# A fused attention and feed-forward block on one core: its calls written out as one list for all engines

## The chip, the cores and the metric

The kernel runs on one core of one Trainium2 chip. The metric is device microseconds of one execution, the median of the runs. A core has TensorE (matmuls; "PE", its weight loads "PEld"), VectorE ("DVE"), ScalarE ("ACT"), GpSimd ("POOL") and SyncE ("SP", which here only issues DMAs). Each engine runs its instructions in the order in which they were written and waits on semaphores for the others. Matmul results land in PSUM, from which VectorE or ScalarE copies them out.

## What is computed

One layer over S = 2048 rows of D = 640, 32 heads of 20 columns, FF = 1536, all in bf16. The inputs, cut to what matters:

```python
h  = x + attention(layernorm(x))
h2 = h + (gelu(n @ w_gate) * (n @ w_up)) @ w_down      # n = layernorm(h)

# attention of x (normalised):
q, k, v = split(x @ wqkv)                               # 32 heads of 20
pq, pk  = q @ w_phi, k @ w_phi                          # per head, 20 x 20
phi_q   = concat(softmax(pq), softmax(-pq))             # 40 features
phi_k   = concat(softmax(pk), softmax(-pk))
kv, z   = sum_s(phi_k^T v), sum_s(phi_k)
o       = (phi_q @ kv) / (phi_q @ z + 1e-6)
return o @ wo
```

## The kernel before

Rows are cut into 16 tiles of 128 (`t`), four tiles make a block (`b`), the 640 columns are five chunks of 128 (`c`).

**Start (lines 169 to 435).** x tiles 0 and 1 are loaded first, then W_v in three parts between the later x tiles. Nine matmuls on zeros warm TensorE up (`warm`, line 212), two more stand in between (`WA`). Each x tile has its mean and variance taken by `ln_stats` (two halves with bn_stats, then bn_aggr). Tiles 0 and 1 are only centred (`ln_0`, line 246): the factor 1/std goes into the later copies of v and into the exponential of k. Tile 3's sums come from ScalarE (`st3_act`). The first six tiles are transposed by TensorE (`transpose_to`, line 142), the others by a DMA transpose on SP's queue. `v_part` and `v_mm` make v; `fold` (line 214) multiplies W_k, and later W_q, with the 20 x 20 matrices of the heads, using the transposed weights that `load_T` fetches by DMA transpose.

**The k stage (lines 440 to 488).** For each tile: `k_tile` makes pk on TensorE and two exponentials (plus and minus) on ScalarE; `v_mm` makes v of tile t+4; `ln_ap` normalises tile t+6 and issues its DMA transpose; `k_norm` (line 310) sums the exponentials on VectorE, takes the reciprocal and multiplies v by it, once per sign, on GpSimd or VectorE (`VP` says which). `kv_tile` (line 334) adds k^T v of a tile into the PSUM tile `kvp`; `KVG` gathers the tiles 0-1, 2-5, 6-9, 10-11, and 12 to 15 follow behind the loop. Four q products stand at t = 15 (`QT`). `kv_mask` brings the sums, masked, into `KV`. PSUM is a pool of four slots at first, then of three and `kvp`.

**After it (lines 493 to 737).** `attn_a` makes numerators and denominators from the exponentials of q, `attn_b` to `attn_b3` divide them, `attn_t` transposes, `attn_c` multiplies with W_o, `attn_d` adds x and takes the sums for the second normalisation, `attn_e` normalises and transposes. `gate_up` makes one of twelve strips of the hidden layer, `down` the output. `weave` mixes the attention steps of later tiles into the list of strips by position.

The order on all engines is thus that of these loops and of `weave`. The first k product (line 274) and the first strip (line 618) are the marks used below.

Of the kernel before, what the change touches and what calls it, by code (L numbers as in the profile page):

```python
# [17 lines left out]
def kernel(  # L18
# [25 lines left out]

    H0 = [(P * c) // Dh for c in range(NC)]
    NH = [(P * c + P - 1) // Dh - H0[c] + 1 for c in range(NC)]
    NWARM = 9
    VP = (0, 2, 4, 6, 9, 11)
    KA, QA = (0, 2, 4), (0, 1, 2, 3, 4)
    FQ = (4, 6, 8, 10, 12)  # L50

    QG = ((0, 1), (2, 3), (4, 5), (6,), (7, 8), (9, 10), (11, 12), (13, 14), (15,), (16,), (17,), (18,), (19,))
    QT = (15, 15, 15, 15)
    WA = 2
    T3 = 4

    KVG = {5: (0, 1), 9: (2, 3, 4, 5), 13: (6, 7, 8, 9), 15: (10, 11)}
    VC = Dh + 1
    KC = Dh + 2


    UH = H // 2
    HALF = (slice(0, 64), slice(64, P))

# [4 lines left out]

    const = ctx.enter_context(tc.tile_pool(name="const", bufs=1))  # L70
    ps_cm = ExitStack()
    psG = ps_cm.enter_context(tc.tile_pool(name="psG0", bufs=4, space=PSUM, reuse_waits="tile"))
    ctx.enter_context(tc.manual_schedule(engines={nc.tensor.engine, nc.sync.engine}))
    man_cm = tc.manual_schedule()
    man_cm.__enter__()
# [6 lines left out]
    KV = const.tile([P, NC, 2, 4, KC], BF16, name="KV")  # L82

    Eq = [const.tile([P, len(g), 2, 512], BF16, name=f"Eq{j}") for j, g in enumerate(QG)]
# [6 lines left out]

    def eq(t, c, s):
        for E, g in zip(Eq, QG):
            if t // 4 * NC + c in g:
                return E[:, g.index(t // 4 * NC + c), s, t % 4 * P:(t % 4 + 1) * P]

    def small(pool, shape, name, bufs=3):
        return pool.tile(shape, F32, name=name, bufs=bufs)

    def gtile(name):  # L100
        return psG.tile([P, 2, 512], F32, name=name, tag="G")

    def ln_stats(pool, tiles, tag, act=True, between=None, log=False):

        n = len(tiles)
        mv = small(pool, [P, n, nc.vector.BN_AGGR_DIM], "mv" + tag)
        stats = small(pool, [P, n, 2, nc.vector.BN_STATS_DIM], "stats" + tag)
        for j, xt in enumerate(tiles):
            for i in range(2):
                nc.vector.bn_stats(stats[:, j, i, :], xt[:, i * HD:(i + 1) * HD])  # L110
                if between and i == j == 0:
                    between()
        for j in range(n):
            nc.vector.bn_aggr(mv[:, j, :], stats[:, j])
        ve = small(pool, [P, n], "ve" + tag)
        rstd = small(pool, [P, n], "rstd" + tag)
        if log:

            nc.scalar.activation(ve, mv[:, :, 1], ACTF.Ln, bias=eps)
            nc.scalar.activation(rstd, ve, ACTF.Exp, scale=-0.5)  # L120
        else:
            nc.gpsimd.tensor_scalar_add(ve, mv[:, :, 1], EPS)
            nc.gpsimd.tensor_tensor(rstd, ve, nhalf[:, 0:n], op=ALU.pow)

        mr = small(pool, [P, n], "mr" + tag)
        if act:
            for j in range(n):
                nc.gpsimd.tensor_scalar(mr[:, j:j + 1], mv[:, j, 0:1], rstd[:, j:j + 1], -1.0,
                                        op0=ALU.mult, op1=ALU.mult)
        return [(xt, mv[:, j, 0:1], rstd[:, j:j + 1], mr[:, j:j + 1]) for j, xt in enumerate(tiles)]  # L130

    def ln_act(pool, tag, xt, mean, rstd, mr):
        ln = pool.tile([P, D], BF16, name="ln" + tag, bufs=3)
        nc.scalar.activation(ln, xt, ACTF.Identity, bias=mr, scale=rstd)  # L134
        return ln

    def ln_dve(pool, tag, xt, mean, rstd, mr):
        ln = pool.tile([P, D], BF16, name="ln" + tag, bufs=3)
        nc.vector.tensor_scalar(ln, xt, mean, rstd, op0=ALU.subtract, op1=ALU.mult)  # L139
        return ln  # L140

    def transpose_to(dst, src, on_pe, on_dve=False):

        if on_pe:
            tp = psG.tile([P, 16, P], BF16, name="tp", tag="G")
            for c in range(NC):
                nc.tensor.transpose(tp[:, c, :], src[:, c * P:(c + 1) * P], ident)  # L147
            (nc.vector.tensor_copy if on_dve else nc.scalar.copy)(dst, tp[:, 0:NC, :])  # L148
        else:
            nc.sync.dma_start_transpose(dst, src)  # L150

# [9 lines left out]

    vS = [p1.tile([P, H, VC], BF16, name=f"vS{i}") for i in range(8)]
    fp_cm = tc.tile_pool(name="fp", bufs=1, side="right", reuse_waits="tile")
    fp = fp_cm.__enter__()
    WkT = fp.tile([P, NC, D], BF16, name="WkT")
    WqT = p1.tile([P, NC, D], BF16, name="WqT")


    nc.gpsimd.memset(nhalf, -0.5)
    nc.gpsimd.memset(eps, EPS)  # L170
    nc.sync.dma_start(x_sb[0][:, 0:1, :], x_v[:, 0:1, :])
    nc.sync.dma_start(x_sb[0][:, 1:2, :], x_v[:, 1:2, :])

    nc.scalar.add_instruction(mybir.InstLoadActFuncSet(name=nc.get_next_instruction_name(), act_func_set_id=6))
    nc.sync.dma_start(Wv[:, 0:2, :], w_v[:, 0:2, 2 * D:3 * D])
    nc.sync.dma_start(x_sb[0][:, 2:3, :], x_v[:, 2:3, :])
    nc.sync.dma_start(Wv[:, 2:4, :], w_v[:, 2:4, 2 * D:3 * D])
    nc.sync.dma_start(x_sb[0][:, 3:4, :], x_v[:, 3:4, :])
    nc.sync.dma_start(wphi, phi_v.rearrange("(c p) f -> p c f", p=P))
    nc.sync.dma_start(Wv[:, 4:5, :], w_v[:, 4:5, 2 * D:3 * D])  # L180
    nc.sync.dma_start(x_sb[1][:, 0:2, :], x_v[:, 4:6, :])

    def load_T(WT, i, *ds):

        for d in ds:
            nc.sync.dma_start_transpose(WT[:, :, d * P:(d + 1) * P], A_wqkv[d * P:(d + 1) * P, i * D:(i + 1) * D])

    load_T(WkT, 1, *range(NC))
    wo_v = A_wo.rearrange("(c p) n -> p c n", p=P)
    wg_v = B_w_gate.rearrange("(c p) n -> p c n", p=P)  # L190
    wu_v = B_w_up.rearrange("(c p) n -> p c n", p=P)


    zero = fp.tile([P, 512], BF16, name="zero")
    nc.vector.memset(zero, 0.0)
    for i in range(8):
        nc.vector.memset(vS[i][:, :, Dh], 1.0)
    make_identity(nc, ident)
    nc.gpsimd.memset(hmask, 1.0)
    for c in range(NC):  # L200
# [3 lines left out]
        nc.gpsimd.affine_select(out=hmask[:, c, :], in_=hmask[:, c, :], pattern=[[Dh, 8]],  # L204
                                compare_op=ALU.is_ge, fill=0.0, base=Dh - 1 - off, channel_multiplier=-1)

    wu = gtile("wu")
    def warm(n):
        for _ in range(n):
            nc.tensor.matmul(wu[:, 0, :], lhsT=zero[:, 0:P], rhs=zero, start=True, stop=True)  # L210

    warm(NWARM)

    def fold(WT, W2, halves, ds=range(NC)):


        runs = []
# [7 lines left out]
        for d in ds:  # L225
            wa = gtile("wa")
            for i, (u, c, a, b) in enumerate(runs):
                nc.tensor.matmul(wa[:, u, a - u * HD:b - u * HD], lhsT=WT[:, c, d * P:(d + 1) * P],  # L228
                                 rhs=BD[:, c].rearrange("p a b -> p (a b)")[:, a - H0[c] * Dh:b - H0[c] * Dh],
                                 start=(i == 0 or runs[i - 1][0] != u),  # L230
                                 stop=(i + 1 == len(runs) or runs[i + 1][0] != u), skip_group_check=True)
            dst, src = W2[:, d, :].rearrange("p (u f) -> p u f", u=2), wa[:, :, 0:HD]
            if halves:
                dst = W2[:, d, :].rearrange("p (c u f) -> p u c f", c=NC, u=2)
                src = src.rearrange("p u (c f) -> p u c f", c=NC)
            if d in (QA if halves else KA):
                nc.scalar.copy(dst, src)
            else:
                nc.vector.tensor_copy(dst, src)

    lnp, Ek, Vt = {}, {}, {}

    CT = (0, 1)
    nrstd = [p1.tile([P, 1], F32, name=f"nrstd{t}") for t in CT]

    def ln_0(t):
        xt, mean, rstd, _ = lnp[t] = ln_stats(p1, [x_sb[0][:, t, :]], f"c{t}", False, None, True)[0]
        nc.gpsimd.tensor_scalar(nrstd[t], rstd, -1.0, None, op0=ALU.mult)
        xc = fp.tile([P, D], BF16, name="xc", bufs=2)
        nc.vector.tensor_scalar(xc, xt, mean, None, op0=ALU.subtract)  # L250
        return xc

    def ln_st(*tiles, act=True, between=None, log=False):
        for t, v in zip(tiles, ln_stats(p1, [x_sb[t // 4][:, t % 4, :] for t in tiles], "1", act, between, log)):
            lnp[t] = v
# [512 lines left out]
```

## Time and profile before

| | |
|---|---|
| median of 3 runs (lowest to highest) | 278.62 us (278.49 to 278.63) |
| span of the profiled execution | 276.6 us |
| first TensorE matmul (warm-up) starts | 1.24 us |
| first transpose of an x tile starts | 5.05 us |
| first v matmul starts | 6.58 us |
| first k matmul starts | 16.99 us |
| last group of k^T v starts | 67.83 us |
| first strip of the hidden layer starts | 90.28 us |
| last store is issued by | 274.39 us |

The span runs from the first to the last instruction of the profiled execution; the time of a run holds what lies around it too, 2.0 us here. The page counts a matmul as busy from its start to its modelled end, so neighbours overlap: in a run of equal matmuls the step from start to start is the figure that adds up. The granted clock is 1.000 in every stretch asked for. An engine that is idle costs nothing unless TensorE, or the end, waits for it.

The large groups of the page, for later comparison: gate and up products 61.9 and 61.7 us busy (line 618), down products 53.8 (line 639), W_o, W_k and W_v products 24.3, 24.0 and 19.8, q products 22.9.

### The profile page before, as it was taken

What the parts mean: (1) busy time and instruction counts of PE and PEld (TensorE: products, weight loads), DVE (VectorE), ACT (ScalarE), POOL (GpSimd) and SP (SyncE); (2) the same over time, 40 slices, a digit from 0 to 9 for tenths busy, and PEclk for the clock granted to TensorE, in tenths of its full rate; (3) what the DMA queues carried; (4) which work ended last, traced back from release to release, by engine and by line L of the source; (5) the groups of instructions that cost most, each with busy time, mean ns of one, the idle gap of its engine ahead of it and who ended that gap; (6) DMA issues with size and microseconds to landing.
All of it is one profiled execution on the core that took longest, in us unless ns stands there. A gap on an engine that the chain in (4) does not pass through costs nothing.

```text
span 276.6 us, 5825 instructions
## 1 busy us (share of the span) xinstructions
PE 271.6 (98%) x2337; PEld 172.5 (62%) x2337; DVE 168.6 (61%) x292; ACT 142.6 (52%) x238; POOL 96.6 (35%) x214
## 2 busy tenths in 40 slices
PE   7999999999999999999999999999999999999995
PEld 3777767765555887788754455675455566444574
DVE  6899999999486875775325667322666622233222
ACT  4779997868598755374524364414445440222200
POOL 4548997765202227275201353300226230000000
DMA  7964634189820022324110213130112613000011
GB/s 215 184 237 86 95 72 97 24 260 393 272 80 0 4 47 47 74 54 72 39 56 2 47 27 70 25 97 24 19 31 29 69 25 95 26 0 0 0 50 47
DMA packets 42235, 21.37 MB, mean 77 GB/s; under 512 B 35040, under 2 KB 40416, under 8 KB 42208
## 3 DMA queue, kind: packets, MB, share of 16 engines
q1 hardware_dynamic: 42208, 21.01, 30.5%
q8 instruction: 18, 0.29, 0.4%
q14 instruction: 9, 0.07, 0.1%
HBM read 10.18 MB, written 2.62 MB: 46 GB/s over the span
## 4 chain that ended last, share of the span: by engine, by line
PE 95%; DMA 1%; ACT 1%; DVE 1%; issue 0%; ACTq 0%; DVEq 0%
PE gu L618 38%; PE pd L639 19%; PE pq L362 8%; PE po L573 8%; PE pk L274 7%; PE pv L274 6%; PE ab L513 3%; PE kvp L340 2%; PE wu L210 1%; DMA LN1T<-ln 1%; PE tp L147 1%; PE pv L290 1%; PE wa L228 1%; ACT E L307 0%; DVE ln L139 0%
## 5 line engine op out<-in xcount | busy, mean ns | idle before, releaser
L624 DVE TENSOR_TENSOR GT<-gu,g 128x512 bf16<-128x512 f32 (+1 forms) x60 | 34.4, 580 | 54.3 <-ACT g L621 54.1
L621 ACT ACTIVATE g<-gu 128x512 bf16<-128x512 f32 (+1 forms) x60 | 30.8, 513 | 69.3 <-PE gu L618 68.4
L618 PE MATMUL gu<-LN2T,Wg 128*128 128x512 bf16 (+1 forms) x300 | 61.9, 337 | 0.1
L618 PE MATMUL gu<-LN2T,Wu 128*128 128x512 bf16 (+1 forms) x300 | 61.7, 336 | 0.0
L639 PE MATMUL pd<-Wd,GT 128*128 128x320 bf16 (+2 forms) x396 | 53.8, 295 | 0.0
L639 PEld LDWEIGHTS <-GT 128*128 128x128 bf16 x396 | 38.0, 98 | 15.3 <-DVE GT L624 0.9
L618 PEld LDWEIGHTS <-Wu 128*128 128x128 bf16 x300 | 29.4, 98 | 22.6
L618 PEld LDWEIGHTS <-Wg 128*128 128x128 bf16 x300 | 28.4, 98 | 20.7
L274 PEld LDWEIGHTS <-LN1T 128*128 128x128 bf16 x290 | 27.8, 98 | 10.8 <-DMA LN1T<-ln 0.4
L322 POOL TENSOR_TENSOR vt<-vS,rs 128x672 bf16<-128x672 bf16 x22 | 29.1, 1345 | 9.1 <-DVE rs L318 6.1
L644 DVE TENSOR_TENSOR y<-pd,x_sb 128x640 bf16<-128x640 f32 (+3 forms) x18 | 13.5, 750 | 30.2 <-PE pd L639 30.2
L521 ACT COPY AB<-ab 128x704 f32<-128x704 f32 x28 | 19.6, 748 | 19.8 <-PE ab L513 19.5
L554 DVE TENSOR_TENSOR tt<-AB,w 128x1280 bf16<-128x1280 f32 x16 | 23.8, 1484 | 1.1 <-POOL w L547 0.9
L573 PE MATMUL po<-Wo,oT 128*128 128x320 bf16 x160 | 24.3, 299 | 0.0
L274 PE MATMUL pk<-Wk,LN1T 128*128 128x320 bf16 x160 | 24.0, 299 | 0.0
L314 DVE TENSOR_REDUCE sk<-E 128x64 f32<-128x1280 bf16 x16 | 22.9, 1434 | 0.2 <-ACT E L307 0.2
L362 PE MATMUL pq<-LN1T,Wq 128*128 128x512 bf16 x100 | 22.9, 379 | 0.0
L367 ACT ACTIVATE Eq<-pq 128x1024 bf16<-128x1024 f32 (+1 forms) x26 | 19.9, 830 | 2.4 <-PE pq L362 2.4
L307 ACT ACTIVATE E<-pk 128x640 bf16<-128x640 f32 x28 | 18.3, 710 | 4.4 <-PE pk L274 4.3
L274 PE MATMUL pv<-Wv,LN1T 128*128 128x320 bf16 x130 | 19.8, 299 | 0.3 <-DMA LN1T<-ln 0.3
L573 PEld LDWEIGHTS <-oT 128*128 128x128 bf16 x160 | 15.6, 98 | 7.0 <-ACT oT L148 0.3
L134 ACT ACTIVATE ln<-x_sb,v,rstd 128x640 bf16<-128x640 bf16 x14 | 12.9, 919 | 11.4 <-POOL v L601 11.2
(102 smaller groups left out, 271.3 us busy)
## 6 DMA issues: line engine op xcount, KB each, us to landing
out_dram<-y SPq DMA_DIRECT2D x15, 160.0 KB, 1.8
Wg<-in_B_w_gate_dram SPq DMA_DIRECT2D x1, 1920.0 KB, 9.2
Wu<-in_B_w_up_dram SPq DMA_DIRECT2D x1, 1920.0 KB, 15.1
Wd<-in_B_w_down_dram SPq DMA_DIRECT2D x1, 1920.0 KB, 8.9
x_sb<-in_A_x_dram SPq DMA_DIRECT2D x2, 640.0 KB, 6.3
Wo<-in_A_wo_dram SPq DMA_DIRECT2D x1, 800.0 KB, 10.8
x_sb<-in_A_x_dram SPq DMA_DIRECT2D x4, 160.0 KB, 3.0
Wv<-in_A_wqkv_dram SPq DMA_DIRECT2D x2, 320.0 KB, 3.9
```

The lines of the kernel that those rows point to most:

```text
L274: nc.tensor.matmul(ps[:, u, 0:HD], lhsT=lnT(t, c), rhs=W[:, c, u * HD:(u + 1) * HD], start=(c == 0), stop=(c == NC - 1))
L314: nc.vector.reduce_sum(sk, Ek[t].rearrange("p s (h f) -> p (s h) f", f=Dh), axis=AX.X)
L322: eng.tensor_tensor(vt[:, s], vS[t % 8], rs[:, s * H:(s + 1) * H, None].to_broadcast([P, H, VC]), ALU.mult)
L362: nc.tensor.matmul(pqs[j][:, i, :], lhsT=Wq2[:, kc, c * P:(c + 1) * P], rhs=LN1T[b][:, kc, :], start=(kc == 0), stop=(kc == NC - 1))
L367: nc.scalar.activation(Eq[j][:, :, s, :], pqs[j][:, 0:len(QG[j])], ACTF.Exp, scale=(1.0, -1.0)[s])
L521: (nc.vector.tensor_copy if u >= 2 - dve else nc.scalar.copy)(AB[:, :, u * UH:(u + 1) * UH].rearrange("p s h f -> p s (h f)"), ab[u][:, :, ...
L554: nc.vector.tensor_tensor(tt.rearrange("p s (h f) -> p s h f", f=Dh), num, w[:, :, :, None].to_broadcast([P, 2, H, Dh]), ALU.mult)
L573: nc.tensor.matmul(po[:, u, 0:HD], lhsT=st[t][:, c, :], rhs=Wo[:, c, u * HD:(u + 1) * HD], start=(c == 0), stop=(c == NC - 1))
L618: nc.tensor.matmul(gu[:, i, 0:n], lhsT=W[:, c, f * P:(f + 1) * P], rhs=LN2T[b][:, c, a0:a1], start=(c == 0), stop=(c == NC - 1))
L621: nc.scalar.activation(g[:, 0:n], gu[:, 0, 0:n], ACTF.Gelu_apprx_tanh)
L624: nc.vector.tensor_tensor(st[b, "g", f][:, a0:a1], gu[:, 1, 0:n], g[:, 0:n], ALU.mult)
L639: nc.tensor.matmul(pd[:, u, n0:n1], lhsT=st[b, "g", f][:, tl * P:(tl + 1) * P], rhs=Wd[:, f, u * HD + n0:u * HD + n1], start=(f == 0), sto ...
```

## The change

The loops, `weave` and the tables of positions are gone. Every step is now a small function, and below them stands one list of some 850 calls, each with its tile and, where there is a choice, its engine ("a" ScalarE, "v" VectorE, "g" GpSimd). All engines run in the order of this list. What differs:

- x tiles 3, 2, 0 and 1 are loaded ahead of W_v. Tile 3 has its statistics by bn_stats on VectorE; tiles 2, 0 and 1 are centred from their sum alone (scaled by -640), and their squares are summed by ScalarE behind it. The factor 1/std of these three goes into the copies of v and the exponentials of k.
- Ten warm-up matmuls, none in between.
- PSUM is four slots by name; a step takes the one whose release was written longest ago, and `kvp` takes one of them like the rest.
- k^T v in three groups: tiles 0-5, 6-9, 10-15.
- Of the 32 multiplies of v, 24 are on GpSimd (22 before).
- Scores are made and copied by sign, not by half of the heads, and their denominators are mostly on VectorE.
- The order of strips, down products, transposes, loads and stores is new throughout; the instructions of the hidden layer are the same.

```diff
-    CT = (0, 1)
+    CT = (0, 1, 2)
...
+    slots, held = [0, 1, 2, 3], {}
+
+    def gtile(name, shape=(P, 2, 512), dtype=F32):
+        g = slots.pop(0)
+        ps = psG.tile(list(shape), dtype, name=name, tag=f"G{g}")
+        held[id(ps)] = g, ps
+        return ps
+
+    def give(ps):
+        slots.append(held.pop(id(ps))[0])
...
+    def c_sum(t, e):
+        need(("x", t))
+        if e == "a":
+            nc.scalar.activation(junk, xt(t), ACTF.Identity, accum_out=col(tsum, t))
+        else:
+            nc.vector.reduce_sum(col(tsum, t), xt(t), axis=AX.X)
...
+    def c_xc(t):
...
+        nc.vector.tensor_scalar(xc[t], xt(t), -float(D), col(tsum, t), op0=ALU.mult, op1=ALU.add)
+
+    def c_sq(t):
+        need(("sum", t))
+        nc.scalar.activation(junk, xt(t), ACTF.Square, bias=col(tsum, t), scale=-float(D), accum_out=col(tsq, t))
...
+    load_x(3, 4)
+    bn(3, 0)
+    bn(3, 1)
+    load_x(2, 3)
+    load_x(0, 1)
+    c_sum(0, "v")
+    c_sum(2, "a")
+    c_xc(2)
+    tr(2)
+    load_x(1, 2)
+    rt(3, 1, "a")
+    ap(3, "v")
+    tr(3)
+    c_sum(1, "a")
+    c_sq(0)
+    c_sq(1)
+    c_sq(2)
+    c_xc(0)
+    tr(0)
+    c_xc(1)
+    tr(1)
+    c_rstd(0, 2)
+    load_v(0, 2)
+    tc_(3, 0, 5, "v")
+    tc_(2, 0, 5, "v")
+    tc_(0, 2, 5, "v")
+    tc_(0, 0, 2, "v")
+    tc_(1, 0, 5, "v")
+    load_v(2, 4)
+    c_rstd(2, 3)
+    load_v(4, 5)
+    vm(3)
+    ve(3)
```

In the list, `load_x`, `load_v`, `load_T`, `load_w`, `dt` (x tiles), `o_dt`, `dt2` (normalised h) and `so` (stores) are SP's; `tr`, `vm`, `km`, `fm`, `kv`, `qm`, `ab`, `po_`, `gu` and `dn` are TensorE's (transposes, v, k, folds, k^T v, q, scores, W_o, strips, down); `ve`, `ke`, `qe`, `gl` are ScalarE's copies and functions; `ks`, `kr` VectorE's sums and reciprocals; `kx` the multiplies of v. SP's order from the first DMA transpose of an x tile up to the weights of the hidden layer:

```diff
+    dt(7)
+    load_x(12, 16)
+    dt(6)
+    load_T(0, 2)
+    load_T(0, 1)
...
+    load_T(0, 4)
+    dt(9)
...
+    dt(8)
...
+    load_T(0, 0)
+    load_T(0, 3)
+    dt(10)
...
+    dt(11)
...
+    dt(12)
...
+    dt(13)
...
+    dt(1)
+    load_w("o")
...
+    dt(14)
...
+    dt(2)
...
+    dt(0)
+    dt(15)
...
+    load_w("u")
+    load_w("g")
```

TensorE's order there, other engines left out: k 0, 1, 3, 2, 4; v 5; k 6; v 6, 7; k 5, 8; v 9, 8, 10; k 9; fold; k 7; fold; k 11; k^T v 0 to 5; k 10; v 12, 13; k 12; v 11; fold; k 13; v 14; k 14; fold; k^T v 6 to 9; fold; v 15; q 0; k 15; q 3, 2, 1; k^T v 10 to 15; q 4.

More of the change, by code (lines that the diff above doesn't have):

```diff
@@ L132, in ln_act @@
[L132 to L150, printed above, removed]
+    epsd = const.tile([P, 1], F32, name="epsd")
@@ L177 @@
[L177 to L188, printed above, removed]
@@ L207, with tr, tc_, dt @@
+    def tr(t):
+        tps[t] = transposes(ln.pop(t) if t in ln else xc.pop(t))
+    def tc_(t, c0, c1, e):
+        copy(e, lnT(t, slice(c0, c1)), tps[t][:, c0:c1, :])
+        have.update(("lnT", t, c) for c in range(c0, c1))
+        if all(("lnT", t, c) in have for c in range(NC)):
+            give(tps.pop(t))
+    def dt(t):
+        nc.sync.dma_start_transpose(lnT(t), ln.pop(t))
+        have.update(("lnT", t, c) for c in range(NC))
+        have.add(("LN", t))
     wu = gtile("wu")
-    def warm(n):
+    def warm(n, i=0):
@@ L501, with qe, loop_pools @@
-    LN2T, st = {}, {}
-    def attn_a_mm(t):
+    def qe(j, s):
+        nc.scalar.activation(Eq[j][:, :, s, :], pqs[j][:, 0:len(QG[j])], ACTF.Exp, scale=(1.0, -1.0)[s])
+        have.update(("q", bc, s) for bc in QG[j])
+        if all(("q", QG[j][0], i) in have for i in range(2)):
+            give(pqs.pop(j))
+    def loop_pools():
+        nonlocal ev, ev_cm
+        fp_cm.__exit__(None, None, None)
+        ev_cm = tc.tile_pool(name="ev", bufs=1, side="right", reuse_waits="tile")
+        ev = ev_cm.__enter__()
@@ new lines, in o_dt, with o_tr, o_tc, po_ @@
+    def o_dt(t):
+        oT[t] = p2.tile([P, NC, P], BF16, name="oT", bufs=3)
+        nc.sync.dma_start_transpose(oT[t], o.pop(t))
+    def o_tr(t):
+        tp2[t, 0] = transposes(o.pop(t))
+    def o_tc(t, e):
+        oT[t] = p2.tile([P, NC, P], BF16, name="oT", bufs=3)
+        copy(e, oT[t], tp2[t, 0][:, 0:NC, :])
+        give(tp2.pop((t, 0)))
+    def po_(t):
+        need(("W", "o"))
+        po[t] = gtile("po")
+        for u in range(2):
+            for c in range(NC):
+                nc.tensor.matmul(po[t][:, u, 0:HD], lhsT=oT[t][:, c, :], rhs=Wo[:, c, u * HD:(u + 1) * HD],
+                                 start=(c == 0), stop=(c == NC - 1))
@@ new lines @@
+    qe(6, 1)
+    o_tr(0)
+    o_tc(0, "a")
+    qe(6, 0)
+    qm(7)
+    qe(7, 0)
+    qe(7, 1)
+    po_(0)
+    res(0, True)
+    qm(11)
+    o_tr(1)
+    o_tc(1, "a")
+    qe(11, 1)
+    qm(8)
+    qe(8, 0)
+    qe(8, 1)
+    qe(11, 0)
+    po_(1)
+    res(1, True)
+    ab(2, 0)
+    ae(2, 0, "a")
+    ab(2, 1)
+    ae(2, 1, "a")
+    qm(9)
+    qe(9, 0)
+    qe(9, 1)
+    qm(10)
+    qe(10, 0)
+    qe(10, 1)
+    ap2(0, "v")
+    tr2(0)
+    tc2(0, "a")
+    qm(12)
+    qe(12, 1)
+    ap2(1, "v")
```

1623 lines of the change are left out of this document (1144 added, 479 removed).

## The prediction

> **What bounds the kernel now.** The view of all cores comes first: one core, 276.6 us, clock 1.000. Then the page: its busy lines, its slices, and the chain that ended last.
>
> ```profile
> PE 271.6 (98%) x2337; PEld 172.5 (62%) x2337; DVE 168.6 (61%) x292; ACT 142.6 (52%) x238; POOL 96.6 (35%) x214
> ...
> PE   7999999999999999999999999999999999999995
> ...
> DVE  6899999999486875775325667322666622233222
> ...
> PE 95%; DMA 1%; ACT 1%; DVE 1%; issue 0%; ACTq 0%; DVEq 0%
> ```
>
> TensorE is both the busy engine and the chain, so the only time to be won lies where the chain leaves it, or where it streams slowly. A busy matmul row overlaps its neighbours, so I read steps, from the chain in order of time:
>
> ```profile
> 1.24 4.02 PE wu L210 x9
> ...
> 8.02 0.93 DVE ln L139
> 9.00 0.45 PE tp L147 x5
> ...
> 29.69 1.36 PE pk L274 x10
> 31.05 0.89 PE kvp L340 x40
> 31.93 1.47 PE pv L274 x10
> ...
> 37.52 3.52 DMA LN1T<-ln
> 41.09 1.53 PE pv L274 x10
> ...
> 55.88 1.65 PE kvp L340 x80
> 57.52 2.82 PE pk L274 x20
> 60.34 7.55 PE pq L362 x35
> 67.90 2.41 PE kvp L340 x120
> ```
>
> Ten matmuls of 320 columns take 1.36 us (0.136 each), of 512 columns 2.16. From 9.00 on TensorE hardly stops. What is left to win: the start up to 9.00; one transposed x tile late at 41.09; and the k^T v groups. Those cost 0.89 for 40 matmuls, 1.65 for 80 and 2.41 for 120, so 0.019 per matmul and 0.13 per group, and the projection behind a group takes 1.47 instead of 1.36: 0.24 per group. Second view, busy time by stage: VectorE is busy 18.89 of 19.16 us between 20.84 and 40.00, 19.48 of 20 up to 60 and 8.56 of 8.70 up to 68.7. In the k stage it keeps up only just.
>
> **The change, part by part.** The matmuls are the same but for one warm-up less (10, not 9 and 2), so I count waits, against 276.6.
>
> *Start.* x tiles 3, 2, 0, 1 are issued first. The loads of the first two tiles land 2.3 and 2.4 us after issue (3.1 and 3.6), and the next two should follow at half a microsecond each: 4.1, 4.6. VectorE then does: statistics of tile 3 (0.89 and 0.21, to 4.26), sum of tile 0, centring of 2 (0.39, row L250), normalising 3 (0.45, row L139), centring of 0 and 1 (0.78), copy of tile 3's transpose (0.49, row L148). The sum is in no row; it lies between nothing and the 1.43 of L314, which reduces twice the elements; I take half, 0.72. That gives 7.2, and the first V product at 7.25. ScalarE's sum of 2 (0.73 and 0.19, row L372) ends at 4.55, and its logarithm and exponential for 3 at 5.1, both before VectorE asks. ScalarE then has four more passes of 0.84 to 0.92 and two more logarithms before the first V copy (from 9.4, where TensorE has finished that tile at 8.6); with four PSUM slots the next three V tiles go on, so that costs nothing while the fifth allocation comes after 11. Ten warm-up steps of 0.42 end at 5.5, and the first centred tile is there at 5.45. W_v's three loads now follow 640 KB of x; in the trace 1280 KB had landed by 7.5 and W_v's last part by 8.1, and the V products of tile 3 read the later parts at 7.8 and 8.35.
> Work up to the first k product: 30 transposes of 0.056, 50 V matmuls, five folds of 0.32, 10.1 us; 1.1 of it is done by 7.25. Before, 7.3 us of work was left at 9.00 and the first k product started at 16.99: 0.67 of small waits. If all of them stay, k now starts at 16.9, if none do, at 16.2. I take 16.74, **-0.25**. If the sum costs 1.43, it is +0.45.
>
> *k stage.* Three groups instead of four: **-0.24**. The wait at 41.09 (0.45 in front of TensorE's weight load, 0.02 in a run without a wait) goes: **-0.43**, if each tile's transpose lands in time. SP is one queue. V of tile 10 waits for a transpose that now stands behind two of W_q's. ScalarE's own work up to that normalisation ends near 29.9, SP is free for it at 31.4, and TensorE asks at 34.8. A transposed x tile lands after 2.6 us, or after 3.8 and 4.2 right behind one of W_q: 34.0 to 35.6. k of tile 8 waits for ScalarE's copy of V 6 to free its PSUM slot: 0.2. I take **+0.2** for the stage, with 0 and 1.1 as its ends. Also, x tiles 12 to 15 are queued behind the transpose of tile 7 (18.8 instead of 12.9); they land 5.0 to 7.6 later, by 23.8 to 26.4, and VectorE asks at 25.4.
>
> *VectorE in that stage.* Tiles 8 to 11 land near 17, and nine half-tile statistics of 0.40, four aggregates of 0.2 and one normalisation end near 22.0. From there to the last multiply: 16 sums with reciprocals at 1.94 from start to start (31.0), 8 multiplies at 0.95 (the trace has 0.76 to 1.4; 7.6), four tiles of statistics (3.9), four normalisations (3.2), one fold copy (0.8): 46.5, done at 68.5. TensorE, at 53.3 less 0.43 and 0.24 from 16.74, asks for it at 69.0. Cost nothing, by half a microsecond. GpSimd's 24 multiplies of 1.31 and its small steps end at some 67.6, asked for at 68.6. Copies of scores, now by sign and not by half, have the same form (128x704, 0.75 and 0.89).
> The row behind those multiplies: normalising on VectorE takes 0.45 with GpSimd idle and 0.95 beside GpSimd's multiplies. [...]
>
> *After the k stage.* The mask chain (0.21, 0.51, 0.90 with handovers, 70.35 to 72.08) stays behind one q product of ten matmuls (2.27): no cost, 0.3 to spare. At 78.2 TensorE lost 0.2 behind the transpose of o; another order of q products fills it: **-0.2**. The 16 score blocks stay 16 groups. Block handover: tile 7's second transpose stands in SP's queue behind the store of tile 3, which waits for that tile's down products; both land some 7.3 us after the output projection of 7, TensorE asks at 8.4. In the last block the third transpose lands at some 10.5, with seven down products (11.4) beside it. Cost nothing; without this cover each would show its excess in full. W_o, W_u and W_g land 9 to 15 us after issue and are asked for over 20 us later. The last matmuls, add and store are the same form: nothing, plus or minus 0.1.
>
> Sum: -0.25 - 0.24 - 0.43 + 0.2 - 0.2 = **-0.9**, a span of 275.7. The median of the runs lies 2.0 above the profiled span (278.62 against 276.6), so **277.7**.
>
> **Rivals.**
> *VectorE becomes the bound of the k stage (slower).* For: its 98% there, and the row means (1.43, 0.55, 1.07) give 48.7 instead of 46.5, with 0.7 idle as in 40 to 68.7 now: 22.0 + 49.4 = 71.4, then one last k^T v tile of 0.4. k^T v would end at 71.8 instead of 70.3, and the start, the groups and the transposed tile are worth nothing: +1.5 - 0.2, 279.9. It decides once those 46.5 exceed 47.0. Against: rows overlap, and start-to-start steps are the shorter ones.
> *Transfers late.* V of tile 10 waits to 35.6 (+0.8) and x tiles 12 to 15 hold VectorE a little: 278.6, no change. For: 3.8 and 4.2 in the trace; against: the two W_q loads may be issued long before.
> *The clock.* The nine warm-up matmuls step at 0.42 us where 512 columns later step at 0.216: half speed until some 5.7. If the thinner stretch from 5.5 to 7.25, transposes alone, kept it there for another such 4.4 us, 2.2 would be lost: 279.9. Against: now too there are transposes and waits between 5.05 and 6.58, and the V products behind them step at 0.136. [...]
> *It does not act.* TensorE is the bound, its work is the same, and every wait removed returns elsewhere: 278.5.
>
> **Chances.** Forecast 0.52, its own range 277.0 to 278.3; VectorE 0.22; transfers 0.16; clock 0.06; no effect 0.04. About 0.2% (0.56 us) is what a measurement of this kernel tells from no change. Faster by more: 0.45 of the forecast's 0.52. Same: its other 0.07, transfers 0.12, no effect 0.04, VectorE 0.01: 0.24. Slower: VectorE 0.21, clock 0.06, transfers 0.04: 0.31. The range, 276.9 to 279.9, reaches from all waits gone to the VectorE case.
>
> **What would show it.** First V product near 7.25 and first k product near 16.7; three k^T v groups, the last ending near 69.6; no wait of TensorE on a transposed x tile; first gate matmul some 0.9 earlier than 90.28; from there to the end 186 us as now. Wrong if k^T v ends after 70.3 with TensorE idle behind VectorE's multiplies, if V products step at 0.27, or if the gap grows after the first gate matmul.

## The result, and the profile after

| | before | changed |
|---|---|---|
| median of 4 runs each, same chip (lowest to highest) | 278.62 us (278.49 to 278.87) | 279.93 us (279.79 to 280.59) |
| span of the profiled execution | 276.6 us | 278.9 us |
| first v product | 6.58 | 7.89 |
| first k product | 16.99 | 18.32 |
| start of the last k^T v product | 70.11 | 72.87 |
| first strip of the hidden layer | 90.28 | 93.44 |

The ratio is 1.0052, interval 1.0035 to 1.0069: slower by half a per cent, where 277.7 had been forecast. The traced run is the slowest of the four (280.59, which is 1.7 above its span), so the trace shows about 0.7 us more than the usual loss.

The table adds up in three pieces: up to the first k product 1.33 lost, from there to the last k^T v product 1.43 lost (54.55 us instead of 53.12), after it 0.48 won (206.02 instead of 206.50). So the loss lies wholly ahead of 73 us. The page of the changed kernel, busy time, TensorE's slices and the shares of the chain:

```profile
PE 271.1 (97%) x2336; PEld 172.3 (62%) x2336; DVE 178.0 (64%) x334; ACT 139.2 (50%) x238; POOL 82.0 (29%) x170
...
PE   7989989999999999999999999999999999999995
...
PE 87%; DMA 5%; SPq 4%; ACT 2%; issue 1%; DVE 0%; ACTq 0%
```

TensorE's busy time is the same to 0.5 us, but of the chain it now has 87% instead of 95%. The DMA's 5% are the waits shown next. SP's 4% are the start: behind the first of these waits the chain goes back over SP's issues, 0.79 to 12.46, where it followed TensorE in the kernel before. Of its slices, 7 us each, the first, the third (14 to 21 us) and the sixth (35 to 42) lie under 9. The chain in order of time says what it waits for:

```profile
11.88 0.58 SPq L150
12.46 0.05 issue
12.51 5.43 DMA WkT<-in_A_wqkv_dram
17.95 0.05 issue
18.00 0.49 PE wa L340 x6
...
33.78 3.18 DMA LN1T<-ln
36.96 0.05 issue
37.00 1.53 PE pv L314 x10
...
49.47 5.59 DMA LN1T<-ln
55.06 0.05 issue
55.11 1.53 PE pv L314 x10
```

Three times the chain leaves TensorE for a DMA transpose: the fifth chunk of W_k, issued right behind the load of x tiles 6 and 7 (line 150), x tile 10, and x tile 14. By the steps of TensorE (the time from one matmul's start to the next, less the usual step) these cost 1.33, 1.02 and 0.66 us, and a fourth, tile 12 at 47.3, 0.38; 3.39 in all. VectorE is no releaser there, and the waits view of TensorE names nobody else behind the start.

### The profile page after: what moved, and what is told of

Same layout as the page of the kernel before. It is cut to its first block, busy times and chain, and to the rows that moved or that the text cites. A ratio compares the mean times of both kernels' runs of the same rounds, so it can differ in the third digit from the quotient of the medians.

```text
span 278.9 us, 5793 instructions
## 1 busy us (share of the span) xinstructions
PE 271.1 (97%) x2336; PEld 172.3 (62%) x2336; DVE 178.0 (64%) x334; ACT 139.2 (50%) x238; POOL 82.0 (29%) x170
## 4 chain that ended last, share of the span: by engine, by line
PE 87%; DMA 5%; SPq 4%; ACT 2%; issue 1%; DVE 0%; ACTq 0%
PE gu L605 38%; PE pd L630 19%; PE po L532 8%; PE pq L434 8%; PE pk L360 6%; DMA LN1T<-ln 3%; PE pv L314 3%; PE ab L478 3%; SPq L162 2%; DMA WkT<-in_A_wqkv_dram 2%; PE kvp L401 2%; ACT E L367 1%; SPq L150 1%; PE wa L340 1%; SPq L154 0%
## 5 line engine op out<-in xcount | busy, mean ns | idle before, releaser
L611 ACT ACTIVATE g<-gu 128x512 bf16<-128x512 f32 (+1 forms) x60 | 29.2, 509 | 70.3 <-PE gu L605 70.3
L618 DVE TENSOR_TENSOR GT<-gu,g 128x512 bf16<-128x512 f32 (+1 forms) x60 | 33.6, 579 | 39.3 <-ACT g L611 39.2
L386 POOL TENSOR_TENSOR vt<-vS,rs 128x672 bf16<-128x672 bf16 x24 | 32.7, 1391 | 3.4 <-DVE rs L380 3.3
L314 PE MATMUL pv<-Wv,LN1T 128*128 128x320 bf16 x160 | 23.7, 299 | 1.6 <-DMA LN1T<-ln 1.6
L124 ACT COPY AB<-ab 128x704 f32<-128x704 f32 x21 | 15.1, 747 | 11.2 <-PE ab L478 5.4
L314 PEld LDWEIGHTS <-LN1T 128*128 128x128 bf16 x160 | 15.2, 98 | 8.2 <-DMA LN1T<-ln 2.6
L360 PEld LDWEIGHTS <-LN1T 128*128 128x128 bf16 x160 | 15.4, 98 | 5.9
L566 POOL TENSOR_SCALAR v<-sm 128x1 f32<-128x1 f32 x14 | 3.7, 264 | 48.8 <-DVE x_sb L553 48.3
```

The source lines that it names most:

```text
L314: nc.tensor.matmul(pv[t][:, u, 0:HD], lhsT=lnT(t, c), rhs=Wv[:, c, u * HD:(u + 1) * HD], start=(c == 0), stop=(c == NC - 1))
L360: nc.tensor.matmul(pk[t][:, u, 0:HD], lhsT=lnT(t, c), rhs=Wk2[:, c, u * HD:(u + 1) * HD], start=(c == 0), stop=(c == NC - 1))
L386: E[e].tensor_tensor(Vt[t][:, s], vS[t % 8], rs[t][:, s * H:(s + 1) * H, None].to_broadcast([P, H, VC]), ALU.mult)
L611: nc.scalar.activation(x[:, 0:a1 - a0], p[:, 0, 0:a1 - a0], ACTF.Gelu_apprx_tanh)
L618: nc.vector.tensor_tensor(GT[b, f][:, a0:a1], p[:, 1, 0:a1 - a0], x[:, 0:a1 - a0], ALU.mult)
```

## The experiments

Two theories stood at the outset. *Q*: the order on SP's queue makes transposes late, and each wait of TensorE is worth its length. *V*: VectorE holds the k stage (it is busy 18.82 of 19.16 us from 20.84 to 40), and a wait removed returns behind it. A third, *F* (instruction packets make transposes late), came out of the first four runs. Every run is compared with runs of the kernel before on the same chip (its medians: 278.45 to 278.62).

| kernel | median us (lowest to highest, runs) | ratio to before, interval | last k^T v |
|---|---|---|---|
| changed | 279.93 (279.79 to 280.59, 4) | 1.0052 (1.0035 to 1.0069) | 72.87 |
| e1: W_k's fifth chunk first | 281.58 (281.14 to 281.76, 4) | 1.0105 (1.0092 to 1.0118) | 73.89 |
| e2: two W_q chunks later | 279.60 (277.44 to 280.23, 12) | 1.0023 (1.0005 to 1.0041) | 72.49 |
| e3: W_o later | 279.71 (279.18 to 280.30, 5) | 1.0039 (1.0027 to 1.0051) | 71.47 |
| e4: all three | 279.69 (278.66 to 282.19, 12) | 1.0043 (1.0025 to 1.0062) | 71.95 |
| e5: and x 12 to 15 early | 279.86 (277.65 to 281.85, 12) | 1.0055 (1.0030 to 1.0080) | 69.92 |
| e6: changed, shorter warm-ups | 281.02 (280.58 to 281.81, 5) | 1.0089 (1.0076 to 1.0102) | 71.78 |
| e7: before, shorter warm-ups | 280.16 (279.85 to 280.81, 5) | 1.0059 (1.0047 to 1.0071) | 71.84 |
| e5 again | 282.34 (1 run) | | 74.58 |
| e8: e5 with slack | 278.38 (277.95 to 280.56, 12) | 1.0003 (0.9987 to 1.0020) | 71.02 |
| e9: and x 6, 7 early | 278.18 (277.36 to 279.25, 12) | 0.9986 (0.9973 to 1.0000) | 70.39 |
| e10: and v of tile 5 early | 278.76 (278.24 to 280.08, 12) | 1.0013 (1.0002 to 1.0024) | 70.99 |
| e11: and tile 8 early | 277.54 (277.41 to 277.89, 6) | 0.9967 (0.9954 to 0.9979) | 70.18 |

**Moving SP's calls one at a time (e1, e2, e3), and all at once (e4).**

```diff
# e1
+    load_T(1, 4)
     load_x(6, 8)
...
-    load_T(1, 4)
# e2
-    load_T(0, 0)
-    load_T(0, 3)
     dt(10)
...
     dt(11)
+    load_T(0, 0)
+    load_T(0, 3)
# e3
-    load_w("o")
...
     dt(15)
+    load_w("o")
     load_w("u")
```

> The changed kernel (279.93 us) with one call moved on SP's queue: the transposed load of W_k's fifth chunk is issued ahead of the load of x tiles 6 and 7 instead of behind it. In the trace of the change that load is issued at 12.51 behind x 6-7 (11.88), lands at 17.95, and TensorE stands for 1.33 us before the last fold of W_k. Theory Q (SP's order makes transfers late, and each wait of TensorE is worth its length): it lands by some 15.5, the wait goes, first k product near 17.0 instead of 18.3, time 278.6 to 278.9. Rival V (VectorE holds the k stage, with x 6 to 11 now landing later still): TensorE waits later for the multiplies or the normalised tiles, time 279.6 to 280.2.

> The changed kernel with the transposed loads of W_q's chunks 0 and 3, which stand ahead of the transpose of x tile 10 on SP's queue, moved behind that of tile 11, where the queue is empty from 37.4 to 43.4. In the trace of the change TensorE stands 1.02 us for tile 10 at 36 to 37. Theory Q: tile 10 lands near 33, the wait goes, k^T v and the first gate matmul come 0.9 to 1.0 earlier, time 278.9 to 279.1. Rival V: the time won is lost again before k^T v of tiles 10 to 15, because VectorE is no earlier: 279.6 to 280.0.

> The changed kernel with the load of W_o moved from ahead of the transpose of x tile 14 (issued 48.03, the transpose 49.47, landed 55.06, 5.59 later) to behind that of tile 15. TensorE stands 0.66 us for tile 14 at 54.3 to 55.1. Theory Q: the transpose lands some 2.6 after issue, by 52.1, the wait goes, time 279.2 to 279.4; W_o, asked for only after 80 us, still lands in time. Rival V: no change, 279.8 to 280.0.

> All three moves of SP's queue in one kernel. Theory Q: the gains add, 1.33 + 1.02 + 0.66 = 3.0, time 276.9 to 277.3, so below the kernel before (278.62); k^T v ends near 70.0 instead of 73.0. Rival V: VectorE, busy 18.8 of 19.2 us between 20.84 and 40, can't follow; TensorE's waits turn into waits for sums and multiplies, k^T v ends at 71.8 or later, time 278.8 to 279.7.

In each trace the wait aimed at is gone: W_k's fifth chunk lands at 15.70 in e1, tile 10 is not waited for in e2, the transpose of tile 14 lands 51.52 in e4, 2.57 after issue. The times hardly follow: by the medians 0.33 and 0.22 us gained in e2 and e3 where 1.0 and 0.65 were expected, 0.24 in e4 where it should have been 3.0 (by the ratios of the table 0.8, 0.4 and 0.25), and e1 lost 1.65. The traced runs took 280.23 us in e2 and 279.18 in e3. But the rest does not go to VectorE. The traces show it at other transfers: in e2 tile 12 costs 0.98 instead of 0.38 and tile 14 0.81 instead of 0.66; in e4 tile 6, behind the load of x 12 to 15, costs 2.03. So theory Q had the kind of wait right and its sum wrong, and theory V does not fit either.

e1's loss has two parts. Its trace is 1.0 us longer than that of the changed kernel, 0.17 up to the first k product and 0.84 from there to the last k^T v product. The 0.84 are transposes again: tiles 6, 10, 12 and 14 cost 0.32, 0.66, 0.83 and 1.10, which is 2.9 instead of 2.06. The start, which should have won 1.33, is something else. The edit concerns a call at 12 us, and the trace differs from 4 us on: x tiles 2 and 0 landed at 3.92 and 5.54 (3.55 and 4.77 in the changed kernel). TensorE's instructions from there, the changed kernel first, then e1 (start, busy time, engine and line, count, idle before):

```profile
5.96 0.45 PE L144 MATMUL tp<-ident,xc 128*128 128x128 bf16 x5 [0.41 <-DVE xc L218]
6.32 0.45 PE L144 MATMUL tp<-ident,ln 128*128 128x128 bf16 x5
...
7.89 4.79 PE L314 MATMUL pv<-Wv,LN1T 128*128 128x320 bf16 x34
```

```profile
6.73 0.71 PE L144 MATMUL tp<-ident,xc 128*128 128x128 bf16 x5 [1.04 <-DVE xc L218]
7.24 0.74 PE L144 MATMUL tp<-ident,ln 128*128 128x128 bf16 x5
...
8.84 5.46 PE L314 MATMUL pv<-Wv,LN1T 128*128 128x320 bf16 x34
```

The same five transposes take 0.71 instead of 0.45 and the same 34 products 5.46 instead of 4.79: from start to start 0.107 and 0.267, twice the usual steps, until 10.17. In the trace's clock records full clock begins at 10.20 in e1 and at 5.28 in the changed kernel. TensorE had stood for 1.25 us beyond its step between the last warm-up and the first transpose. The first k product came at 18.49 where e4, with the same calls up to there, had 16.78: 1.7 us. That is the rival of the clock in the prediction, and it hid what e1's edit did at the start. The wait alone does not bring it: in e10's trace TensorE was idle longer there (1.7 us by the waits view, 1.04 in e1) and has full clock from 4.06. In the changed kernel the record of full clock is 273.066 us long, 80 times 3.413 (the length of the record of half clock in e5's second trace, below), and in every other trace that has such records they are whole multiples of 3.413 us long too; where they begin differs from trace to trace (5.28, 10.20 and 4.06 above). That this beginning, and so luck, decided in e1 is the author's guess, not shown. The three other runs of e1 were not traced; that they lost the same way is only likely from their times.

**What makes a transpose late that has nothing ahead of it (e6, e7).** In the changed kernel the transpose of tile 12 took 3.83 us though SP's queue had been empty for 4.7. The DMA records hold, beside the program's own packets, packets of kind "instruction": in each trace 18 of 16 KB on queue 8, 0.88 to 1.76 us long. From one to the next TensorE starts 253 matmuls and weight loads in the mean in the changed kernel and 251 in the kernel before. The first four of the changed kernel fall at 15.40, 31.24, 44.51 and 53.19, and each of these lies inside a late transpose or ahead of one. Theory F says that they are the cause. If they come by the count of TensorE's instructions, cutting the warm-up matmuls in four moves them and leaves SP's order as it is.

```diff
-            nc.tensor.matmul(wu[:, 0, :], lhsT=zero[:, 0:P], rhs=zero, start=True, stop=True)
+            for j in range(4):
+                nc.tensor.matmul(wu[:, 0, j * P:(j + 1) * P], lhsT=zero[:, 0:P], rhs=zero[:, j * P:(j + 1) * P],
+                                 start=True, stop=True)
```

> The changed kernel (279.93 us) with its ten warm-up matmuls of 512 columns cut into forty of 128: the same columns, 60 more instructions of TensorE at the start, nothing else. The DMA records hold 16 KB packets of kind 'instruction' on queue 8, one for every 256 or so instructions of TensorE; in the trace of the change they fall at 15.40 (1.51 us long), 31.24 (1.37), 44.51 (1.12) and 53.19 (0.88), each inside a transpose that TensorE then waited for. Theory F (these packets make a transpose in flight about as much later as they are long): with 60 instructions more they come 60 instructions earlier, near 13.1, 27.3, 44.0 and 49.6. The two W_q transposes issued near 30 and 31 land some 3 us after issue instead of 4.6 and 4.9, tile 10 lands by 36.0, its wait of 1.02 shrinks to 0.3 or less; the one at 44 stays where it was, inside the transpose of tile 12. Time 278.9 to 279.4. Theory Q alone (only what stands ahead on SP's queue counts): the W_q transposes take 4.6 and 4.9 as before, time 279.8 to 280.2.

> The kernel before (278.62 us) with the same edit: its eleven warm-up matmuls of 512 columns cut into 44 of 128. Theory F: the instruction packets, now at 28.64, 42.53 and 48.90, come near 25, 38.3 and 45.4. The x tile transpose issued at 27.47, which took 3.83, takes 2.6; the one at 37.52, which took 3.52 and made TensorE wait 0.43 at 41.09, takes up to 4.7 and the wait grows by up to 1.1; those near 40.4 and 43.3 are touched or left free. Time 278.6 to 279.8 where TensorE had no slack, and the landing times move as said in any case. Theory Q alone: landing times and the time as before, 278.5 to 278.8.

e7 is the clearest run of all: the kernel before loses 1.6 us by an edit that gives TensorE the same columns at the start. That is more than theory F had put on it (up to 279.8), since the packet met a transpose that the expectation had not named. Its chain, then that of the kernel before in the same place:

```profile
24.99 4.90 DMA LN1T<-ln
29.89 0.05 issue
29.94 1.53 PE pv L276 x10
```

```profile
26.66 1.36 PE pk L274 x10
28.02 0.32 PE wa L228 x6
28.33 1.36 PE pv L274 x10
```

A transpose issued at 24.99 lands 4.90 later, where the one at 24.82 in the kernel before took 2.58; TensorE stands 1.60 us. (The traced run, of 280.81, loses 0.7 more at a transpose of o at 132 us.) The DMA view of e7 from 26.1 to 27.8 (busy share of the 16 DMA engines in 40 slices, then the queues with packets, MB and share):

```profile
DMA  0947999999999999999990000000000000001000
...
q8 instruction: 1, 0.02, 5.4%
```

One instruction packet starts in it (at 26.15; at 28.64 in the kernel before) and takes 5.4% of 16 engines for 1.7 us, that is one engine for 1.47 us; the transposes' data run dry at 27.1, and the other 15 engines stand to 27.8. The wait at 41.09 of the kernel before did not grow as expected: that transpose took 3.47 (3.52 before), and TensorE waited 0.38 instead of 0.43 for it.

e6 confirms where it aimed: with the packet at 26.45 instead of 31.24 the two W_q transposes take 2.88 and 3.34 instead of 4.59 and 4.86. But the packet now sits in the transposes ahead of these. Tile 9's takes 3.60 and holds SP for 2.20 instead of 1.20, so that tile 8's, asked for first, lands at 31.53 and costs 1.01; tile 10's is issued at 32.90, takes 3.37, and still costs 0.65. Its waits of TensorE (line, whom it waited for, us, times, longest):

```profile
PE pv L316 <- DMA LN1T<-ln: 1.0, 2, 0.5
PE pk L362 <- DMA LN1T<-ln: 0.8, 1, 0.8
PE po L534 <- DMA oT<-o: 0.8, 1, 0.8
PE gu L607 <- DMA LN2T<-ln: 0.6, 1, 0.6
```

The last two are behind the first strip, where the changed kernel had no such wait; that shifted packets met these transposes of o and of normalised h is the author's reading of it. So F alone is as incomplete as Q alone.

e6 also settles the fifth chunk of W_k. It stands behind x tiles 6 and 7 as in the changed kernel, but with the packet at 10.93 instead of 15.40 it lands at 16.40, 3.40 after its issue instead of 5.43, and TensorE does not wait for it. The 1.33 took both, the place in the queue and the packet; either one removed (the place in e1 and e4) was enough.

Over all fourteen traces, the transposes of x tiles by what else was there (a packet of queue 8 running between 1.0 us after issue and 0.3 before landing; a plain load issued earlier and not yet landed):

| | number | median us to landing | lowest to highest |
|---|---|---|---|
| neither | 107 | 2.59 | 2.56 to 3.52 |
| plain load ahead | 21 | 3.14 | 2.57 to 5.19 |
| instruction packet inside | 43 | 3.81 | 2.60 to 4.90 |
| both | 9 | 4.44 | 3.71 to 6.42 |

Two things hide in these rows. Queue 14 carries instruction packets too, nine of 8 KB in each trace, 0.31 to 0.83 us long. Of the 107 transposes in the first row, ten have such a packet inside and take 3.29 in the median (2.94 to 3.52); the other 97 take 2.59. The 3.52 behind the wait at 41.09 of the kernel before and the 3.18 of tile 10 in the changed kernel are among the ten. No run moves these packets by themselves, so that they are the cause is not shown. And for a plain load ahead: where it landed 2.3 us or more after the transpose was issued, with no packet of queue 8 inside, the transpose landed 0.6 to 0.8 us behind it.

**The last loads in order (e5, twice).**

```diff
# e5, on e4
     load_x(8, 12)
+    load_x(12, 16)
...
     dt(7)
-    load_x(12, 16)
```

> The three moves of SP's queue and a fourth: the load of x tiles 12 to 15 goes directly behind that of 8 to 11, ahead of the first DMA transpose of an x tile, as in the kernel before. With three moves alone (279.69 us) TensorE stood 2.03 us at 24.8 for x tile 6, whose transpose was issued at 22.18 behind the load of 12 to 15 (21.44, landed 26.11) and landed at 26.92. Theory Q (order on SP's queue): tile 6 lands by 24.9, at most 0.3 of that wait is left, last k^T v product some 1.7 earlier than 71.95, time 277.7 to 278.2. Rival V (VectorE holds the stage): TensorE waits for VectorE's or ScalarE's results at 26 to 40 instead, time 279.2 to 279.8.

> The kernel of the four moves of SP's queue once more, for a second trace: its runs lay between 277.65 and 281.85 us, and the profiled one was the fastest (span 275.9, TensorE waiting once, 0.57 us for tile 12 at 44.97). Theory F and Q together (transposes with under 1 us of slack meet an instruction packet or another transfer in some runs and not in others): in a run of 279 us or more, the extra time is again waits of TensorE for transposes with small slack (tile 8: 0.16, tile 12: none, tile 13: 0.66, tile 15: 0.90), or late x tiles at the start. Rival: the extra time lies after the first gate matmul, in waits that this trace does not have.

The traced run of e5 did what Q says and more: tile 6 landed at 23.64 and was asked for at 24.90, one wait of 0.57 was left (tile 12), k^T v ended at 69.92 and the span was 275.9, the 275.7 of the forecast almost. But its runs spread over 4 us, and the second trace, of a run of 282.34, says why. The window view (PE busy, then the other engines, PEclk, DMA share, GB/s):

```profile
30.50:33.00 2.50, 0.34 (x3) 0.01 (x1) 2.50 (x4) 1.48 (x3) 2.50 (x3) 1.00 0.94 79
33.00:36.00 3.00, 2.91 (x12) 1.66 (x13) 2.93 (x8) 0.06 (x1) 3.00 (x4) 0.53 0.01 0
36.00:39.00 3.00, 3.00 (x22) 2.08 (x21) 2.80 (x3) 3.00 (x5) 2.74 (x7) 0.90 0.01 3
```

TensorE is idle from 30.54 to 33.09, 2.41 us beyond its step, for tile 8: its slack was 0.16 in the first trace, and here an instruction packet at 30.52 made its transpose take 4.46. Then the granted clock is 0.53, and the k products step at 0.267 instead of 0.136 until 36.6. One transpose with no slack cost 2.4 us and then about 1.7 more. The three longest of e5's twelve runs (281.67 to 281.85) have a mean granted clock of 0.993 or 0.994 too, as this run (0.994), and the other nine 0.999 or 1.000. That the time goes before the first strip (95.14 instead of 90.48) rules out the rival of the expectation.

**Slack instead of luck (e8 to e11).** A packet of queue 8 lay inside 52 of the 180 transposes of the table, but a transpose that is asked for 1.3 us later than it needs to land can bear one of median effect (3.81 less 2.59). Of calls that move in e10 and e11, only the new place is shown.

```diff
# e8, on e5
+    mr(8)
+    ap(8, "a")
+    ke(4, 0)
+    dt(8)
     mr(9)
     ap(9, "a")
-    ke(4, 0)
-    load_T(0, 4)
-    dt(9)
-    mr(8)
-    ap(8, "a")
...
     vm(5, by_chunk=False)
-    dt(8)
+    dt(9)
...
     load_T(0, 3)
+    load_T(0, 4)
...
+    vm(11, by_chunk=False)
     vm(12, by_chunk=False)
     vm(13, by_chunk=False)
+    ve(11)
...
-    vm(11, by_chunk=False)
...
-    ve(11)
# e9, on e8
+    load_x(6, 8)
     load_T(1, 1)
+    ve(1)
+    vm(4)
     fm(1, 1)
     fc(1, 1, "a")
-    ve(1)
-    vm(4)
     ve(4)
     load_T(1, 4)
-    load_x(6, 8)
# e10, on e9
+    tr(5)
+    tc_(5, 0, 5, "a")
     vm(4)
...
+    vm(5, by_chunk=False)
     fm(1, 4)
...
     fc(1, 4, "a")
+    ve(5)
# e11, on e10
+    mr(8); ap(8, "a"); dt(8)
     ke(4, 1)
     ke(3, 0)
```

> The four moves, and slack for the two tiles that have least: tile 8, which TensorE asks for first, is normalised and transposed ahead of tile 9; V of tile 11, whose transpose landed 12 us before, goes ahead of V of tile 12; the transposed load of W_q's chunk 4 goes behind chunk 3's. Theory F and Q: tile 8 has 1.4 us of slack, tile 12 has 1.3, no wait of TensorE for a transpose between 17 and 61 us over 0.3, last k^T v product at 69.2 to 69.7, time 277.0 to 277.9, most runs below 278.5, so below the kernel before. Rival V: VectorE and ScalarE are then the bound, TensorE waits for their copies or multiplies, and the median stays at 279 or more.

> The kernel with the four moves and the slack (278.38 us), where TensorE no longer waits for a transpose but 1.07 us at 42.7 and 0.34 and 0.24 later for multiplies of v, and the chain of waits runs over VectorE and GpSimd from 17.8, where x tiles 6 and 7 arrive, to 70.8. Here the load of x 6 and 7 goes ahead of W_k's chunks 1 and 4 on SP's queue, and the fold of chunk 1 goes behind V of tile 4 on TensorE. Theory V (with the transposes on time VectorE and GpSimd are the bound): x 6 and 7 land by 14 instead of 17.8, the first sum on VectorE starts at 22.5 to 23.5 instead of 24.8, the waits for multiplies shrink from 1.65 to 0.6 or less, last k^T v product by 70.2 instead of 71.0, time 277.2 to 277.8, below the kernel before (278.6). Rival: W_k's chunks 1 and 4 now land after TensorE asks, the first k product slides from 16.6 to 17.5 or later, and the time stays at 278.2 to 279.

> The last kernel (278.18 us, span of its profile 276.4) waits once more than at the start: 1.09 us at 16.5 to 17.6 for the fifth chunk of W_k, issued at 12.44 and landed at 17.58 with an instruction packet of 1.76 us at 14.51 inside. Nothing is moved on SP's queue here; V of tile 5 with its copies, now between k of tile 4 and k of tile 6, is done ahead of that fold, so that TensorE has 1.36 us of work while it waits. Theory Q: the wait goes (at most 0.3 left, and up to 0.3 for the transpose of tile 5, done earlier), k^T v ends at 69.3 to 69.8 instead of 70.4, time 277.0 to 277.5, below the kernel before by 0.4% (278.5). Theory V: the multiplies hold TensorE from 42 on, the last k^T v product stays at 70.2 or later, time 278.0 to 278.4.

> In the last kernel (278.76 us, span of its profile 277.0) the wait for W_k's fifth chunk shrank from 1.09 to 0.36, and a new one of 1.10 stood at 32.1: the transpose of tile 8, issued at 27.92, met the instruction packet of 30.05 and landed at 32.07, 4.15 after issue, where the kernel before it (packet at 30.87, issue 27.09) had 2.57. Here the normalising of tile 8 on ScalarE and its transpose go ahead of three exponentials (tile 4's two and the second of tile 3). Theory F and Q: issued near 26.7, it lands by 29.4, ahead of the packet; the wait goes, time 277.5 to 278.0. Theory V (VectorE holds the stage by then): last k^T v product stays at 70.6 or later in spite of it, time 278.4 to 278.8.

In e8 TensorE no longer waits for any transpose, and there rival V appears at last. Its waits behind the start:

```profile
PE kvp L401 <- POOL vt L386: 0.9, 1, 0.9
PE kvp L401 <- DVE vt L386: 0.2, 1, 0.2
```

The chain up to the last k^T v tile is then VectorE's and GpSimd's: from the first sum (24.81; 24.89 in the chain) to 70.80, 45.9 us. On TensorE 1.65 us show as steps too long. e9 gives VectorE its x tiles earlier (first sum at 23.59 instead of 24.81): these waits vanish, as V says, and the rival comes true as well, W_k's fifth chunk lands at 17.58 (a packet at 14.51, 1.76 long) and costs 1.09. Its median of 278.18 can't be told from the kernel before, since the interval ends at 1.0000. e10 fills that wait to 0.36, and its time is not better, for the work moved ahead brings the packet 0.8 us earlier (30.05 instead of 30.87) and tile 8's transpose 0.8 us later (27.92 instead of 27.09), and the two meet:

```profile
27.92 4.15 DMA LN1T<-ln
32.07 0.05 issue
32.12 1.53 PE pk L360 x10
```

With tile 8's transpose ahead of three exponentials (e11) it is issued at 27.03 and lands 2.57 later, and all six runs lie between 277.41 and 277.89. The page of e11, and its waits for a transfer:

```profile
PE 270.9 (98%) x2336; PEld 172.4 (62%) x2336; DVE 177.9 (64%) x334; ACT 138.8 (50%) x238; POOL 82.4 (30%) x170
...
PE 93%; SPq 4%; DMA 2%; issue 0%; DVE 0%
```

```profile
PE wa L340 <- DMA WkT<-in_A_wqkv_dram: 0.7, 1, 0.7
```

The chain is TensorE's again, the span 276.2, and one wait of 0.84 (in TensorE's steps) is left. This version beats both kernels: 0.9967 of the kernel before, interval 0.9954 to 0.9979, and 2.4 us below the changed one across chips.

Of the times expected ahead, only e11's came true for the reason given. Those of e2 and e4 lie in theory V's ranges, though the waits that V names are not in their traces; the others lie outside every range given.

## Why the prediction was wrong, step by step

In the trace the change lost 1.33 up to the first k product (forecast -0.25), lost 1.43 in the k stage (forecast -0.47) and won 0.48 behind it (forecast -0.2). Both misses are transfers that came late.

- **Start, -0.25.** Its own working was off, and its sum came out right by luck. x tiles 0 and 1 landed at 4.77 and 6.16, not 4.1 and 4.6, the sum took 0.82 (0.72), the first v product came at 7.89 (7.25), and the waits behind absorbed it: with W_k in time the first k product starts at 16.78, 16.75 and 16.62 in e4, e5 and e8 (17.10 in e5's second trace), forecast 16.74. What failed is a term that was not there. "Work up to the first k product" counts TensorE's instructions and no transfer, though the fifth transposed load of W_k had been moved past that of x 6 and 7 on SP's queue. There an instruction packet (15.40) met it, and it cost 1.33; with the same order and the packet elsewhere (e6) it cost nothing.
- **k stage, +0.2 with ends 0 and 1.1.** This is the step that failed: "A transposed x tile lands after 2.6 us, or after 3.8 and 4.2 right behind one of W_q". It was worked out for tile 10 alone, and its upper end, 1.1, covered that tile. Measured: tile 10 1.02, tile 12 0.38, tile 14 0.66, together 2.06, with landings 3.18, 3.83 and 5.59 after issue. Tile 10 was late by its issue: 33.78 instead of 31.4, of which 1.33 is the loss of the start, and the rest the second W_q load, which held SP for 2.26 instead of 1.28 while a packet ran (31.24 to 32.61). And the reading of the two rows was wrong: the transposes of 3.83 and 4.23 in the kernel before have instruction packets inside (28.64, 42.53), and others right behind a W_q load (22.23, 33.39 and 46.15) took 2.6, so the W_q neighbour does not explain them. The wait for V 6's PSUM slot, which made up the 0.2, does not show.
- **W_o, W_u and W_g "are asked for over 20 us later".** True of W_o itself, which was in time everywhere. What was not asked is what stands behind it: the transpose of tile 14 landed 2.0 us after W_o (55.06, 53.04), and with W_o behind it 2.57 after its issue (e4). With W_o ahead and no packet of queue 8 inside it took 5.19 (e6), 0.6 behind W_o; in the changed kernel the packet at 53.19 lies between.
- **Three k^T v groups, -0.24.** Right. The steps into and out of the last group are 0.09 and 0.11 longer than others, and there are three. With the old wait at 41.09 gone (-0.43), the k stage gives 2.06 - 0.43 - 0.2 = 1.43, which is what the marks show.
- **VectorE, 46.5 us from 22.0.** The length was right, 45.9 for the chain of e8. The start was not: x 8 to 11 landed at 19.53, not near 17, and the first sum began at 23.93. At that it would have ended near 69.8, so it did not decide in the changed kernel; it does decide once the transposes are in time and the x tiles late (e8). The 0.95 "beside GpSimd's multiplies" was the mean of two rows, 1.47 beside a multiply and 0.43 beside none. Two more multiplies on GpSimd did not make VectorE's slower: the eight left on VectorE took 1.10 in the mean, the ten before 1.08.
- **After the k stage, -0.2.** Measured -0.48 from the last k^T v product to the end. The gap at 78.2 is gone (0.2), two of 0.08 in the down products as well; the rest was not traced further. The 186 us from the first strip became 185.5, and one score group more stands ahead of it.
- **The rivals.** "Transfers late" was the case, with 3.39 us of waits against the 0.8 that it had been priced at. "The clock" did not touch the changed kernel (full clock from 5.28) but took 1.7 us in e1. The range ended 0.03 below the median, and that it came so near is luck: its upper end was the price of VectorE as the bound, which was not the cause.

So the forecast of 277.7 was near what the new order does when its transposes are in time: 277.54 in e11. Only the number agrees, for e11 still waits 0.84 at the start and moves other calls too. The order was judged by what each engine has to do, and the one queue that all transfers share was followed for a single tile. Not tried by themselves were the PSUM slots by release and the scores by sign; no wait in the traces points to them, which does not show that they cost nothing.

## What to carry to other kernels

When calls are reordered, write SP's queue out once with issue and landing of every transfer, and give each the slack to the instruction that asks for it; with less than 1.2 us, the median delay by one packet here, it can be late in some runs (the longest delay was 2.3), and a mean of landing times hides that. A kernel's steady time can rest on where instruction packets happen to fall: in e7 an edit that only changes the number of TensorE's instructions moved one from 28.64 to 26.15 and cost 0.6% (1.0059), so a gain or loss of half a per cent should be read from the waits and not from the time. Waits of TensorE of 1.25 and 2.41 us, in e1 and e5's second trace, were followed by matmuls at twice their usual step, which cost 1.7 us more in each; those in e10 (1.7 us at the start) and e4 (2.03) were not.

## What the runs showed of the hardware

- **Transposes with an instruction packet inside landed later.** The packets of queue 8 have 16 KB and took 0.88 to 1.76 us, 18 in each trace, and that of e7 at 26.15 took one DMA engine for 1.47 us of its window. The transposes of x tiles with one inside landed after 3.81 us instead of 2.59 (medians above), and after 3.29 with one of the 8 KB packets of queue 14 inside. In e7 TensorE stood 1.60 us for one.
- **In one trace the clock fell after a wait of 2.5 us, and returned 3.4 us later.** In e5's second trace the clock record has 0.5 for 3.413 us from 33.17 on (the window view has 0.53 for 33.00 to 36.00 and 0.90 for 36.00 to 39.00), after 2.55 us without a matmul; 2.16 us in e4 (24.80 to 26.96) did not do it. Whether the length of the wait or its place decided, these two traces cannot tell.
- **The page's clock row is silent about the start.** It prints 9 and the window view 1.00 where e1's transposes stepped at 0.107 and its v products at 0.267 up to 10.17. There only the steps tell.
